# Low parts of x and of weight sums on VectorE instead of GpSimd in eleven steps of an FFT-and-feed-forward kernel

## The chip, the cores and the metric

The kernel runs on one core of a Trainium2 chip. The metric is the device time of one execution in microseconds (us). The engines are named as in the profile: PE is TensorE (PEld its weight loads), ACT is ScalarE, DVE is VectorE, POOL is GpSimd, SP is SyncE, which here issues all DMAs.

## The reference

```python
X = np.fft.rfft(x, axis=1)                     # x: 8 x 3008 x 256
Yr = Xr @ w_r - Xi @ w_i + b_r
Yi = Xr @ w_i + Xi @ w_r + b_i
Y  = soft threshold of Yr and of Yi by 0.01
y  = np.fft.irfft(Y, n=3008, axis=1)           # 8 x 3008 x 256
h  = y.reshape(24064, 256) @ w_in              # w_in: 256 x 2048
out = (h - np.tanh(h)) @ w_out                 # w_out: 2048 x 256
```

## The kernel before

All products run in fp32r. Where one product is not exact enough, a number is split: a high part, cast to fp32r by ACT, and a low part, the number minus its high part. The function `split_into` does this; its last argument names the engine of the low part, and GpSimd is what it takes if nothing is said. The product is then three matmuls: low by high, high by high, high by low.

The transform over 3008 points is done as 64 by 47 points, batch by batch. F1 is the first short transform of a batch. For batch 1 (`Forward`), F1 is done in 16 steps of four matmuls' worth of x each; the last eight of them need x split. A step of F1 has a split (`split`, two slots ahead of its use) and a `part`: three matmuls of 94 x 512, which write a PSUM bank, and a copy by ACT (L278) to `st`, which a DMA writes out.

The feed-forward part works on chunks of 512 tokens. The first three chunks (the first pass) go through a loop of steps g, called slots here. The slots that matter are 31 to 43; 44 begins the main phase. A slot does, in this order of the program:

1. `rise`: six matmuls (L594) into a PSUM bank `he`, the tanh by ACT (L597), the subtraction h - tanh(h) by DVE (L598), which reads `he`, and the cast of its high part by ACT (L599, `ghe`).
2. What the list `slots` holds for this slot, by rank: the F1 part (rank 7), the split of x for the F1 two slots on (8.5), a weight step (9), and where one is due, the stacked table (9, behind the weight steps).
3. `finish`: the low part `gle` by DVE (L603).
4. `fall`: six matmuls (L619) with `ghe` and `gle` of two slots ago.

There are two `he` banks. An F1 part takes one of them too, so that in slots 35 to 42 every `rise` writes the same bank, and its matmuls wait until L598 of the slot before has read it. Every engine runs its own instructions in this order.

`weight_sums(p)` prepares, for each of four groups p, sums of blocks of w_in that the main phase (L698, tile `sum`) uses in place of the blocks. It has four steps: `one` (three additions, DVE), `two` (two more by DVE, and the split of one sum), `three` (the split of a second sum, two operations of DVE), `four` (the split of the third sum, a subtraction by DVE, and the split of its result into the tile `weights`). Groups 0 to 2 stand in slots 33 to 36, 36 to 39 and 39 to 42; group 3 stands in slots 43, 44, 45 and 49. In slots 36 and 39, step four of one group and step one of the next fall together.

The stacked table is a table of the DFT that batches 3 and later use; it is loaded by a DMA and split by three small operations of DVE (L333, L334, L335). Its `f1s_h`, the `ws` tiles of the weight sums and the tile `spare` (L653, an operand that POOL prepares for the main phase from slot 41 on) take turns in four buffers.

Of the kernel before, what the change touches and what calls it, by code (L numbers as in the profile page):

```python
# [78 lines left out]
def spectral_ffn(ctx, tc, x, w_r, w_i, b_r, b_i, w_in, w_out, x_twice, f1, f1s, f2, f2_first, i1, i2, out):  # L79
    nc = tc.nc  # L80
    P = 128
# [16 lines left out]
    def split_into(hi, lo, src, rest=nc.gpsimd):  # L98
        nc.scalar.copy(out=hi, in_=src)  # L99
        rest.tensor_tensor(out=lo, in0=src, in1=hi.bitcast(F32), op=ALU.subtract)  # L100
        return hi, lo
# [236 lines left out]
    def rows(t, jp):  # L338
        return t.rearrange("a (g j) d -> a g (j d)", j=NJ)[:, :, 2 * jp * D:(2 * jp + 2) * D]

    class Spectrum:
# [113 lines left out]
        def put(self, pz):  # L455
            zo = work.tile([P, 512], F32, name="zo", tag="tmp", bufs=4)
            nc.scalar.copy(out=zo, in_=pz)
            nc.sync.dma_start(out=rows(z_dram[self.b], self.jp), in_=zo)
# [60 lines left out]
    def h(t):  # L519
        return t.bitcast(F32)  # L520
# [233 lines left out]
    def weight_sums(p):  # L754
        wv = [weights[p // 2][:, v].rearrange("p (k q i m) -> p k i q m", k=2, i=2, m=P)[:, :, :, 2 * (p % 2):2 * (p % 2) + 2] for v in range(2)]
        pair = [work.tile([P, 2, 2, P], F32, name=f"ws{k}", tag="tmp", bufs=4) for k in range(2)]
        t = [v[:, k] for v in pair for k in range(2)]

        def whole(dst, k, i):
            nc.vector.tensor_tensor(out=dst, in0=h(wv[0][:, k, i]), in1=h(wv[1][:, k, i]), op=ALU.add)  # L760

        def op(dst, a, b, how):
            nc.vector.tensor_tensor(out=dst, in0=a, in1=b, op=how)

        def put_sum(i, src):
            split_into(*(v[:, 2 * p * P:(2 * p + 2) * P].rearrange("p (q m) -> p q m", m=P) for v in sums[i]), src)

        def one():
            whole(t[0], 0, 1)
            whole(t[2], 0, 0)  # L770
            whole(t[1], 1, 1)

        def two():
            op(t[1], t[0], t[1], ALU.add)
            op(t[0], t[2], t[0], ALU.subtract)
            put_sum(2, t[0])

        def three():
            put_sum(0, t[1])
            op(t[3], t[1], t[2], ALU.subtract)  # L780
            whole(t[2], 1, 0)

        def four():
            put_sum(1, t[3])
            op(t[2], t[2], t[3], ALU.subtract)
            split_into(wv[0][:, 0, 1], wv[1][:, 0, 1], t[2])

        return one, two, three, four

# [27 lines left out]
    sums = []  # L817
# [3 lines left out]
    def zero_slot(c):  # L821
        return LAST + 2 + 2 * NP2 * (c - FIRST)

    def busy(slot, us):
        load_at[slot] = load_at.get(slot, 0.0) + us

    def plan_spectrum(b, at, offsets, ahead, earliest):
        shared, cross, shrink, inverse = offsets
        done_at[b] = at[-1] + inverse
        for jp, k in enumerate(at):  # L830
            s = Spectrum(b, jp)
            put(max(k - ahead, earliest), 0, s.load)
            if b > 2:
                put(k - 3, 0.7, s.fix)
            for slot, rank, fn, us in (
                (k, 6, s.dft, 1.8), (k + shared, 4, s.shared, 0.7), (k + cross, 3, s.cross, 1.4),
                (k + shrink, 2, lambda s=s: [s.shrink], 0.3), (k + inverse, 2.5, s.inverse, 0.7),
            ):
                put(slot, rank, fn)
                busy(slot, us)  # L840
            if shared == cross:
                busy(k + shared, 9.0)

    def plan_forward(f, slot, *q):
        if len(q):
            put(slot - 1, 0.5, f.split, *q)
        else:
            put(slot - 2, 8.5, f.split)
        put(slot, 7, f.part, *q)
        busy(slot, 0.8)  # L850
        busy(slot - 1, 0.1)

    def calmest(lo, hi, n, us):
        found = sorted(sorted(range(lo, hi + 1), key=lambda k: (load_at.get(k, 0.0), k))[:n])
        for k in found:
            busy(k, us)
        return found

    def prepare(c):
        chunk = chunks[c]  # L860
        at = zero_slot(c)
        if c > FIRST:
            put(at - 15, 0, chunk.unspill)
        tight = c == first_chunk[1]
        put(at - 4 if tight else at - 5, 9, chunk.sums, 0)
        put(at - 3 if tight else at - 4, 0.9 if tight else 9, chunk.sums, 1)
        put(at - 3, 1, chunk.operands, "t3", "b11", "t2", "b21")
        put(at - 2, 1, chunk.operands, "t1")
        put(at - 2, 9, chunk.sums, 2)
        put(at - 1, 1, chunk.operands, "b22", "t4")  # L870
        busy(at - 3, 1.0)
        busy(at - 1, 0.6)
# [8 lines left out]
    def plan():  # L881
        for p, steps in enumerate(WEIGHT_STEPS):
            for k, at in enumerate(steps):
                put(at, 9, weight_step, p, k)
        put(38, 0, share)
        put(36, 0, table_load)
        put(39, 9, stacked_table)
        put(40, 0, first_spares)
        put(42, 0, operand_tiles)
        put(45, 0, more_operand_tiles)  # L890
        for c in range(FIRST, NCH):
            prepare(c)
        for k, at in enumerate(FIRST_F1):
            ch, q = LOOK + k // 2, k % 2
            if q == 0:
                put(at - AHEAD_F1, 0, following[ch].load)
            put(at - 2, 8.5, following[ch].split, q)
            put(at, 7, following[ch].part, q)
            busy(at, 0.9)
        plan_spectrum(1, SPECTRUM_1, (1, 1, 2, 4), 5, SPECTRUM_1[0] - 2)  # L900
        spectra = [None, None]
        for b in range(2, B):
            zs = zero_slot(first_chunk[b])
            spectra.append(zs - (SHIFT_2 if b == 2 else 89))
            plan_spectrum(b, [spectra[b] + 6 * k for k in range(NJ // 2)], (2, 3, 4, 7), 7, spectra[b] - 3)
        for b in range(2, B):
            zs = zero_slot(first_chunk[b])
            if b == 2:
                at = calmest(F1_2, spectra[b] - 5, NP // 2, 0.8)
            else:  # L910
                first = spectra[b - 1]
                at = [first + 1] + [first + 5 + 6 * k for k in range(12)] + [zs - 111 + 4 * (k + 1) for k in range(3)]
                for k in at:
                    busy(k, 0.8)
            for ch in range(NP // XC if b == 2 else 0):
                f = Forward(b, ch)
                put(at[2 * ch] - 3, 0, f.load)
                for q in range(XC // 2):
                    plan_forward(f, at[2 * ch + q], q)
            for k in range(NP // 2 if b > 2 else 0):  # L920
                f = Stacked(b, 2 * k)
                put(max(at[k] - 6, at[k - 3] - 1 if k > 2 else 0), 0.6, f.load)
                plan_forward(f, at[k])
        for c in range(FIRST + 1, NCH):
            units = [Unit(g // 8, g % 8) for g in range(-(-CT * c // 376), -(-CT * (c + 1) // 376))]
            late = [u for u in units if c == first_chunk[u.b]]
            early = [u for u in units if c != first_chunk[u.b]]
            for some_units, window in ((early, (-14, -9 if late else -6)), (late, (-10, -6))):
                at = unit_slots(c, 2 * len(some_units), window, max([done_at.get(u.b, 0) + 2 for u in some_units], default=0))
                for u in some_units:  # L930
                    mine = [at.pop(0) for _ in range(2)]
                    last_two.append(mine[-1])
                    put(max(mine[0] - 5, 48, done_at.get(u.b, 0) + 1, last_two[-3] + 1), 0, u.load)
                    for k, slot in enumerate(mine):
                        put(slot, 8, u.time, k)
# [18 lines left out]
    def weight_step(p, k):  # L954
        if not sums:
            sums.extend([piece(i + 3 * v, [P, FF // 2], F32R, f"sum{i}_{v}") for v in range(2)] for i in range(3))
        if k == 0:
            wsteps[p] = weight_sums(p)
        wsteps[p][k]()
# [34 lines left out]
    with tc.manual_schedule(engines={E.PE, E.Activation, E.DVE, E.Pool, E.SP}):  # L994
# [27 lines left out]
        for i in range(len(steps) + 1):  # L1022
# [3 lines left out]
            if i < len(steps):  # L1026
                f, q = steps[i]
                f.dft(q)
            if i >= 1:
                f, q = steps[i - 1]  # L1030
# [40 lines left out]
        following = [Forward(1, ch) for ch in range(NP // XC)]  # L1071
# [117 lines left out]

        ready, half = {}, {}  # L1190
        plan()

        def rise(g):
# [119 lines left out]
```

## Time and profile before

| what | value |
|---|---|
| median of 3 runs | 2569.62 us (2569.45 to 2571.41) |
| the profiled execution | 2569.43 us |
| its span (first to last instruction) | 2567.6 us |
| mean granted clock of TensorE | 0.999 of full speed |
| PE busy | 2544.6 us of the span, 99% |
| DVE, ACT, POOL busy | 1837.7, 1598.1 and 787.1 us |

The span is 1.8 us shorter than the execution's own time; this part lies outside of the instructions. A PE that is busy for 99% of the span leaves 23 us in which it stands still.

### The profile page before, as it was taken

The page shows a single profiled execution, that of the slowest core. Times are in us where ns is not written, and L with a number is a line of the kernel's source. Part 1 is how long each engine was busy: PE and PEld are TensorE (multiplying, and loading weights), DVE is VectorE, ACT ScalarE, POOL GpSimd, SP SyncE. Part 2 cuts the span into 40 slices and gives each one's busy share as a digit, 9 for nine tenths or more (in the row PEclk, how much of TensorE's full clock was granted, in tenths as well). Part 3 has the DMA queues.
Part 4 walks back from the last instruction along what each step waited for, and adds up shares of the span by engine and source line. Part 5 has one row for each costly group of instructions (what it writes and reads, how often), then busy time and mean ns, then how long its engine had stood idle before and what let it go on. Part 6 is the DMA issues. An engine that isn't in the chain of part 4 may idle for free.

```text
span 2567.6 us, 42817 instructions
## 1 busy us (share of the span) xinstructions
PE 2544.6 (99%) x16000; PEld 2271.5 (88%) x16000; DVE 1837.7 (72%) x2741; ACT 1598.1 (62%) x2926; POOL 787.1 (31%) x881
## 2 busy tenths in 40 slices
PE   9999999999999999999999999999999999999999
PEld 6787988999899998999989899899998999999998
DVE  6788875777767777777776777767777666666665
ACT  5556567666666666666666666666666555565555
POOL 0004335232343332433333333333333223221210
PEclk9999999999999999999999999999999999999999
DMA  6521224232333332323323242233333121111000
GB/s 181 163 83 53 87 92 125 93 107 86 102 107 105 122 102 86 114 86 123 101 86 117 87 129 91 87 116 103 114 94 96 64 66 60 47 43 47 19 27 17
DMA packets 144528, 232.94 MB, mean 91 GB/s; under 512 B 12096, under 2 KB 85952, under 8 KB 144320
## 3 DMA queue, kind: packets, MB, share of 16 engines
q1 hardware_dynamic: 144320, 230.20, 28.8%
q8 instruction: 127, 2.08, 0.3%
q14 instruction: 81, 0.66, 0.1%
HBM read 139.45 MB, written 87.56 MB: 88 GB/s over the span
## 4 chain that ended last, share of the span: by engine, by line
PE 95%; DVE 2%; ACT 1%; DMA 1%; issue 0%; POOL 0%; SPq 0%; ACTq 0%; POOLq 0%; DVEq 0%
PE o L619 39%; PE H L698 34%; PE ps_v L403 5%; PE ps_i L545 4%; PE ps_f L376 3%; PE ps_t L403 2%; PE he L594 2%; PE ps_f L314 1%; PE ps_i L452 1%; PE ps_i L450 1%; PE ps_i L451 1%; PE oe L619 1%; PE ps_f L258 0%; PE ps_v L485 0%; DVE the L598 0%
## 5 line engine op out<-in xcount | busy, mean ns | idle before, releaser
L619 PE MATMUL o<-gh,weights 128*128 128x512 f32 x2816 | 886.2, 396 | 0.0
L742 ACT CAST gh<-th 128x1024 fp32r<-128x1024 f32 x353 | 371.5, 1053 | 382.2 <-DVE th L737 252.9
L698 PEld LDWEIGHTS H<-y_t,sum 128*128 128x128 f32 x3168 | 516.4, 188 | 102.7 <-DVE th L737 5.7
L619 PE MATMUL o<-gl,weights 128*128 128x512 f32 x1408 | 554.4, 394 | 0.0
L698 PE MATMUL H<-y_t,sum 128*128 128x256 f32 x3168 | 548.5, 281 | 0.3
L747 DVE TENSOR_TENSOR gl<-th,gh 128x1024 fp32r<-128x1024 f32 x353 | 440.6, 1249 | 57.1 <-ACT gh L742 54.0
L619 PEld LDWEIGHTS o<-gh,weights 128*128 128x128 f32 x2816 | 442.0, 188 | 14.9
L737 DVE TENSOR_TENSOR th<-H,th 128x1024 f32<-128x1024 f32 x353 | 428.4, 1214 | 5.3 <-ACT th L733 2.3
L733 ACT ACTIVATE th<-H 128x1024 f32<-128x1024 f32 x353 | 362.5, 1027 | 41.3 <-PE H L698 40.8
L714 DVE TENSOR_TENSOR H<-H,late 128x256 f32<-128x256 f32 x352 | 152.2, 432 | 317.3 <-PE H L698 281.5
L698 PE MATMUL H<-y_b,weights 128*128 128x256 f32 x2112 | 361.5, 279 | 0.0
L619 PEld LDWEIGHTS o<-gl,weights 128*128 128x128 f32 x1408 | 264.8, 188 | 60.0 <-DVE gl L747 0.6
L698 PE MATMUL H<-y_more,weights 128*128 128x256 f32 x2112 | 308.7, 281 | 1.2 <-DVE H L720 1.2
L698 PEld LDWEIGHTS H<-y_b,weights 128*128 128x128 f32 x2112 | 298.5, 188 | 0.2 <-POOL y_b L100 0.2
L698 PEld LDWEIGHTS H<-y_more,weights 128*128 128x128 f32 x2112 | 282.3, 188 | 15.9 <-DVE H L720 1.9
L720 DVE TENSOR_TENSOR H<-H,late 128x256 f32<-128x256 f32 x352 | 151.7, 431 | 191.0 <-PE H L698 182.8
L706 ACT COPY late<-H 128x256 f32<-128x256 f32 x352 | 131.6, 374 | 213.1 <-PE H L698 210.1
L100 POOL TENSOR_TENSOR z_l<-mn,z_h 128x512 fp32r<-128x512 f32 x84 | 112.7, 1342 | 431.6 <-ACT z_h L99 277.1
L440 DVE TENSOR_TENSOR y<-tb,ps_v 64x256 f32<-64x256 f32 x384 | 160.7, 418 | 50.5 <-PE ps_v L403 44.0
L100 POOL TENSOR_TENSOR s_l<-xi,s_h 128x256 fp32r<-128x256 f32 x84 | 62.8, 748 | 319.0 <-ACT s_h L99 319.0
L309 POOL TENSOR_TENSOR x<-x,x 64x512 fp32r<-64x512 f32 x55 | 71.4, 1298 | 254.2 <-ACT x L303 105.2
L707 ACT COPY H<-H 128x256 f32<-128x256 f32 x352 | 125.7, 357 | 11.2
(194 smaller groups left out, 3590.3 us busy)
## 6 DMA issues: line engine op xcount, KB each, us to landing
a<-st SPq DMA_DIRECT2D x168, 192.0 KB
x<-in_x_twice SPq DMA_DIRECT2D x55, 512.0 KB
z<-zo SPq DMA_DIRECT2D x96, 256.0 KB
zin<-z SPq DMA_DIRECT2D x64, 384.0 KB
out<-ot SPq DMA_DIRECT2D x46, 512.0 KB
at<-a SPq DMA_DIRECT2D x84, 256.0 KB
shared<-a SPq DMA_DIRECT2D x60, 256.0 KB
shared<-in_i SPq DMA_DIRECT2D x58, 235.0 KB
```

The lines of the kernel that those rows point to most:

```text
L100: rest.tensor_tensor(out=lo, in0=src, in1=hi.bitcast(F32), op=ALU.subtract)
L403: nc.tensor.matmul(dst, lhs[:, t], rhs[:, t, :], start=n == 0, stop=n == 5)
L440: nc.vector.tensor_tensor(out=y[ri * 64:(ri + 1) * 64, jj, :], in0=common(jj, ri), in1=self.vv[jj * 64:(jj + 1) * 64, ri * D:(ri + 1) * D] ...
L619: nc.tensor.matmul(self.o[t][:, :n], lhs, rhs, start=f == 0 and k == 0, stop=f == NF - 1 and k == 2,)
L698: nc.tensor.matmul(dst, a, b, start=start and k == 0, stop=k == 2, skip_group_check=True)
L706: nc.scalar.copy(out=self.p7, in_=self.c11)
L714: nc.vector.tensor_tensor(out=self.c21, in0=self.acc, in1=self.p7, op=ALU.add)
L720: nc.vector.tensor_tensor(out=self.c22, in0=self.acc, in1=self.p7, op=ALU.add)
L733: nc.scalar.activation(out=self.th[:, s], in_=self.hp[:, s, :n], func=AF.Tanh)
L737: nc.vector.tensor_tensor(out=self.th[:, s], in0=self.hp[:, s, :self.n], in1=self.th[:, s], op=ALU.subtract)
L742: nc.scalar.copy(out=self.gh[:, s], in_=self.th[:, s])
L747: nc.vector.tensor_tensor(out=self.gl[:, s], in0=self.th[:, s], in1=h(self.gh[:, s]), op=ALU.subtract)
```

## The change

```diff
+        rest = nc.gpsimd if p == 3 else nc.vector
...
         def put_sum(i, src):
-            split_into(*(v[:, 2 * p * P:(2 * p + 2) * P].rearrange("p (q m) -> p q m", m=P) for v in sums[i]), src)
+            split_into(*(v[:, 2 * p * P:(2 * p + 2) * P].rearrange("p (q m) -> p q m", m=P) for v in sums[i]), src, rest)
...
         def four():
             put_sum(1, t[3])
             op(t[2], t[2], t[3], ALU.subtract)
-            split_into(wv[0][:, 0, 1], wv[1][:, 0, 1], t[2])
+            split_into(wv[0][:, 0, 1], wv[1][:, 0, 1], t[2], rest)
...
         put(38, 0, share)
-        put(36, 0, table_load)
-        put(39, 9, stacked_table)
+        put(27, 0, table_load)
+        put(31, 9, stacked_table)
...
             if q == 0:
                 put(at - AHEAD_F1, 0, following[ch].load)
-            put(at - 2, 8.5, following[ch].split, q)
+            put(at - 2, 8.5, following[ch].split, q, None, nc.vector)
             put(at, 7, following[ch].part, q)
```

Twenty subtractions go from POOL to DVE: eight low parts of x (slots 33 to 40), and for groups 0 to 2 nine low parts of sums and three of `weights`. The table is loaded in slot 27 and split in slot 31, in place of 36 and 39. Lines below the first edit move by two: L760 becomes L762, L763 becomes L765.

On DVE, slot 36 (step four of group 0 and step one of group 1) stood so before, from the L598 of its own `rise` to the next:

```order
L598 TENSOR_TENSOR the_978<-he0_973,the_978 128x512
L763 TENSOR_TENSOR ws1_1731<-ws1_1731 128x256
L760 TENSOR_TENSOR ws0_1827<-weights0_78 128x256
L760 TENSOR_TENSOR ws1_1828<-weights0_78 128x256
L760 TENSOR_TENSOR ws0_1827<-weights0_78 128x256
L603 TENSOR_TENSOR gle_982<-the_978,ghe_980 128x512
L598 TENSOR_TENSOR the_978<-he0_973,the_978 128x512
```

The same slot of the change:

```order
L598 TENSOR_TENSOR the_978<-he0_973,the_978 128x512
L100 TENSOR_TENSOR x_1_5_1_l_1824<-xt_1707,x_1_5_1_h_1823 94x512
L100 TENSOR_TENSOR sum1_1_1734<-ws1_1738,sum1_0_1733 128x256
L765 TENSOR_TENSOR ws1_1738<-ws1_1738 128x256
L100 TENSOR_TENSOR weights0_78<-ws1_1738,weights0_78 128x2x128
L762 TENSOR_TENSOR ws0_1832<-weights0_78 128x256
L762 TENSOR_TENSOR ws1_1833<-weights0_78 128x256
L762 TENSOR_TENSOR ws0_1832<-weights0_78 128x256
L603 TENSOR_TENSOR gle_982<-the_978,ghe_980 128x512
L598 TENSOR_TENSOR the_978<-he0_973,the_978 128x512
```

Three subtractions of L100 stand between the two L598; each reads a high part that ACT casts in this slot.

On ACT the order is the same before and after. This is slot 36 of the change, from its tanh to the next:

```order
L597 ACTIVATE the_978<-he0_973 128x512
L599 CAST ghe_980<-the_978 128x512
L278 COPY st_1820<-he1_974 96x512
L99 CAST x_1_5_1_h_1823<-xt_1707 94x512
L99 CAST sum1_0_1733<-ws1_1738 128x256
L99 CAST weights0_78<-ws1_1738 128x2x128
L597 ACTIVATE the_978<-he0_973 128x512
```

Nothing moved here; the casts that the three subtractions read stand behind L599 and L278.

On POOL, the queue of the change holds behind the one early operation of the preparation (L132) at once the operands of the main phase:

```order
L132 TENSOR_TENSOR w2_f_256<-wi_f_125,wr_f_124 128x512
L653 TENSOR_TENSOR spare_1950<-raw_960 128x256
L653 TENSOR_TENSOR raw_960<-raw_960 128x256
L653 TENSOR_TENSOR spare_1950<-raw_960 128x256
L100 TENSOR_TENSOR y_t3_2009<-spare_1950,y_t3_2009 128x256
```

Before, 18 low parts stood ahead of the first L653, and two more between the second and the third.

## Rows read from the trace of the kernel before

**Rows 1.** Windows: length, then busy us and instructions by engine, clock, DMA.

```profile
200.00:250.00 50.00, 44.65 (x191) 33.98 (x190) 41.92 (x68) 30.07 (x63) 25.65 (x27) 1.00 0.17 48
250.00:300.00 50.00, 48.35 (x329) 44.22 (x328) 39.97 (x68) 30.06 (x60) 16.02 (x19) 1.00 0.30 96
300.00:2500.00 2200.00, 2197.35 (x14260) 1989.39 (x14259) 1561.14 (x2262) 1392.09 (x2543) 738.20 (x822) 1.00 0.29 90
```

**Rows 2.** Waits of PE in 180 to 310 us: total us, times, longest us.

```profile
PE he L594 <- DVE the L598: 4.2, 3, 1.7
```

**Rows 3.** Timeline of DVE, 196 to 262 us: start us, us, instruction [idle before].

```profile
207.06 0.69 DVE L598 TENSOR_TENSOR the<-he,the 128x512 f32<-128x512 f32 x1 [0.32 <-ACT the L597]
207.66 0.68 DVE L212 TENSOR_TENSOR weights<-w_m,weights 128x512 fp32r<-128x512 f32 x1
...
217.63 0.69 DVE L598 TENSOR_TENSOR the<-he,the 128x512 f32<-128x512 f32 x1 [1.09 <-ACT the L597]
...
219.09 1.08 DVE L760 TENSOR_TENSOR ws<-weights 128x256 f32<-128x256 f32 x3
220.10 0.68 DVE L603 TENSOR_TENSOR gle<-the,ghe 128x512 fp32r<-128x512 f32 x1
...
223.73 2.47 DVE L603 TENSOR_TENSOR gle<-the,ghe 128x512 fp32r<-128x512 f32 x1
...
231.84 1.98 DVE L334 CAST f1s_h<-f1s_f 128x48 fp32r<-128x48 f32 x1
...
235.65 0.41 DVE L763 TENSOR_TENSOR ws<-ws 128x256 f32<-128x256 f32 x1
236.09 0.42 DVE L763 TENSOR_TENSOR ws<-ws,ws 128x256 f32<-128x256 f32 x1
236.44 0.68 DVE L603 TENSOR_TENSOR gle<-the,ghe 128x512 fp32r<-128x512 f32 x1
...
245.07 0.69 DVE L598 TENSOR_TENSOR the<-he,the 128x512 f32<-128x512 f32 x1 [1.27 <-ACT the L597]
```

**Rows 4.** Timeline of POOL, 190 to 262 us.

```profile
223.54 1.41 POOL L100 TENSOR_TENSOR x_l<-xt,x_h 94x512 fp32r<-94x512 f32 x1
224.92 0.73 POOL L100 TENSOR_TENSOR sum<-ws,sum 128x256 fp32r<-128x256 f32 x1
...
241.36 0.73 POOL L653 TENSOR_TENSOR spare<-raw 128x256 f32<-128x256 f32 x1
```

**Rows 5.** Timeline of ACT, 196 to 262 us: slot 36.

```profile
218.36 0.62 ACT L599 CAST ghe<-the 128x512 fp32r<-128x512 f32 x1 [0.76 <-DVE the L598]
218.88 0.58 ACT L278 COPY st<-he 96x512 f32<-96x512 f32 x1
219.36 0.62 ACT L99 CAST x_h<-xt 94x512 fp32r<-94x512 f32 x1
219.88 0.41 ACT L99 CAST sum<-ws 128x256 fp32r<-128x256 f32 x1
```

**Rows 6.** Line L100 by engine, DVE: min, median, max ns, first and last start.

```profile
L100 DVE TENSOR_TENSOR x_l<-xt,x_h x2: 682/686/690, 81.4 to 87.6; 94x512 fp32r<-94x512 f32 x2
L100 DVE TENSOR_TENSOR f_l<-f_f,f_h x1: 255/255/255, 4.4 to 4.4; 94x96 fp32r<-94x96 f32 x1
```

**Rows 7.** Timeline of PE, 196 to 262 us.

```profile
213.19 0.40 PE L619 MATMUL o<-gle,weights 128*128 128x512 f32 x1
...
218.80 1.09 PE L594 MATMUL he<-yh,weights 128*128 128x512 f32 x4
...
222.28 1.08 PE L594 MATMUL he<-yh,weights 128*128 128x512 f32 x4
...
245.82 1.20 PE L594 MATMUL H<-yh,weights 128*128 128x512 f32 x4
```

**Rows 8.** Timeline of PE, 19 to 36 us: the end of its longest wait.

```profile
26.50 2.63 PE L376 MATMUL ps_f<-f_f,at 128*128 128x128 f32 x16 [3.81 <-DMA at<-a_first]
```

**Rows 9.** A window of 1 us (columns as in rows 1), behind that wait.

```profile
28.00:29.00 1.00, 1.00 (x7) 1.00 (x6) 0.42 (x1) 0.25 (x1) 0.00 (x0) 0.50 0.67 163
```

## What is expected of the change, and why

> **What bounds the kernel now.** I read the windows first, to see where PE stands still. The 50 us from 200 us on hold 44.65 us of PE work, so 5.35 us of idle PE; the next 50 us hold 48.35; the following 2200 us lack only 2.65 us [rows 1]. From 300 us on PE is the bound, and an idle microsecond of PE ahead of it moves the end by a microsecond. The change lies in 200 to 250 us. Then the waits: 4.2 us of this idle time are three waits of the `rise` matmuls (L594) for DVE's L598, the longest 1.7 us [rows 2]. That is the single `he` bank of slots 35 to 42: the next `rise` can't write before L598 has read. So I follow L598 and call the time from one L598 to the next a round. Slots 33 to 42 are ten rounds, from 207.06 to 245.07 (eleven L598 in all): 38.01 us [rows 3]. The matmuls of the main phase's first `rise` start at 245.82, 0.75 behind the last of these L598 [rows 7]. Whatever the ten rounds gain or lose, the end does too.
>
> How long must a round be? PE needs 3.48 us for a slot with F1: from one `rise` at 218.80 to the next at 222.28, with nothing idle between [rows 7]. Several rounds of before are longer, and the DVE timeline shows why: a subtraction that mostly takes 0.68 us takes 2.47 at 223.73 [rows 3], while POOL is busy with a subtraction from 223.54 and the next one to 225.65 [rows 4]; it ends at 226.20, about one normal duration behind POOL. L334, a cast of 128x48, takes 1.98 [rows 3].
>
> **The change, part by part.**
>
> *Removed.* The stretching by POOL goes. If nothing took its place, PE would get back at most the 4.2 us of waits for L598 [rows 2].
>
> The Trainium skill, page "SBUF — State Buffer", section "Who interferes with whom", says that a DVE instruction with two SBUF inputs contends with a GpSimd instruction that reads SBUF, and that the loser blocks fully. The rows on 223.73 agree. By that rule alone the change is a gain; it is the first rival below.
>
> *Added.* Twenty subtractions on DVE. Eight are 94x512: two such on DVE have a median of 686 ns [rows 6], and behind an instruction of that width the next starts after 0.60 (207.06 to 207.66) [rows 3]. Twelve are 128x256; 0.34 each, a third of the 1.01 from the three L760 to L603 (219.09 to 220.10) [rows 3]. As work this is 8 x 0.60 + 12 x 0.34 = 8.9 us in ten rounds. But the price is not the work. Each subtraction reads a high part that ACT casts late in the same slot, and now DVE waits for it, with L603 and the next L598 queued behind. On POOL nobody waited.
>
> How late ACT is, I read from slot 36, whose L598 starts at 217.63 [rows 3]. ACT then starts L599 at 218.36, the F1 copy at 218.88, the cast of x at 219.36 and the cast of the sum at 219.88 [rows 5]. Counted from L598 that is +0.73, +1.25, +1.73 and +2.25. The cast of x takes 0.62, so it ends at +2.35; with 0.03 to hand over, the low part of x starts at +2.38 and DVE goes on at +2.98. Before, DVE went on to its weight step at once. A cast of 256 columns takes 0.41 [rows 5]; a weight operation that reads the result of the one before starts 0.44 behind it and takes 0.41 (235.65, 236.09) [rows 3]. With that each new round, every handover 0.03:
>
> - Step three (slots 35, 38): the cast of the sum is done by +2.66, so the low part runs at once; 2.98 + 0.34, then 0.44 + 0.34 for its two operations, 0.60 for L603: 4.70.
> - Step two (37, 40): 2.98 + 0.44, the second operation done at 3.83, cast of the sum to 4.27, low part from 4.30 to 4.64, L603: 5.24.
> - Steps four and one together (36, 39): 2.98 + 0.34 = 3.32, the subtraction done at 3.73, cast for `weights` to 4.17, low part from 4.20 to 4.54, three additions 1.01, L603: 6.15.
> - Slot 33 (step one; a weight cast stands where the F1 copy does later): 3.02 + 1.01 + 0.60 = 4.63. Slot 34 (step two, no F1 copy): 0.48 less than in 37, so 4.76.
> - Slot 41 (three, no x left): cast of the sum from +1.73 to 2.14, low part to 2.51, 0.78, L603: 3.89. Slot 42 (four): 2.51, done at 2.92, cast to 3.36, low part to 3.73, L603: 4.33.
>
> Sum: 4.63 + 4.76 + 2 x 4.70 + 2 x 5.24 + 2 x 6.15 + 3.89 + 4.33 = 49.79 us, against 38.01: **+11.8 us**. All these rounds are longer than PE's 3.48, so none of it is covered by PE's work. The tanh that L598 also needs is no later than this: PE may start the next `rise` 0.75 behind L598 [rows 7], and ACT is free again when the last cast is done, one L603 and more ahead.
>
> *Moved: the table.* In slot 39 its three operations cost 1.98 us and more, which is in the 38.01 already. In slot 31 they stand ahead of L603 and L598, where POOL is idle. Upper bound: three times the 255 ns of a subtraction twice as wide [rows 6], 0.77; lower bound 0. I take half: **+0.4**. The DMA of the table is issued in slot 27, four slots ahead; I cost it at nothing, hidden behind those slots.
>
> *Freed: POOL.* L653 now stands first in POOL's queue and waits only for its tile `spare`, whose buffer is given up in slot 38. So three L653 of 0.73 each [rows 4] come about slot 38 or 39 and can hold up DVE there: 0 to 2.2 us. DVE idles for ACT in most of that time, so I take one of them: **+0.7**.
>
> Together 11.8 + 0.4 + 0.7 = 12.9. On the profiled execution's 2569.43 us (0.2 below the median of the runs) this gives **2582.3 us**, 0.5% slower.
>
> **The rivals.**
>
> *Faster: DVE doesn't wait for ACT.* If the casts were ready when DVE reaches them, a round would be its own work: step three 0.60 + 0.60 + 0.34 + 0.44 + 0.34 + 0.60 = 2.92, below PE's 3.48, and the 4.2 us of waits go, less 0.4 for the table: 2565.6. It decides at rounds of 3.48. For it speaks the stretching [rows 3, 4]. Against it, x is cast behind L599 and the F1 copy, which the change doesn't move; L599 itself can't start before L598 ends. Chance 0.07.
>
> *Partly covered.* The waits overlap more than I count, or the 1.65 us that PE idles in 250 to 300 us [rows 1] and later idle time is absorbed by the delay. If a round lost half of what I say, +6 us: 2575.5; near zero if more. Chance 0.10, half of it within 0.2% of before, which is about what a measurement of this kernel can tell from no change (5 us).
>
> *Slower still: TensorE's clock falls.* Its slots 33 and 34 pass at PE's pace, since there the `he` banks still alternate; then PE meets the first long round. PE's last `fall` of slot 35 began its last matmul at 213.19 [rows 7]; with 0.4 for the table and 0.4 for that matmul it is through at 214.0, while the new L598 of slot 35 starts at 207.06 + 0.4 + 4.63 + 4.76 = 216.85 and frees the bank 0.75 later, at 217.6: a wait of 3.6 us. Before, behind a wait of 3.81 us that ended at 26.50 [rows 8] the granted clock was 0.50, the 1.2 GHz level, from 28 to 29 us [rows 9]. One such dip is covered: the `rise` of 1.4 us becomes 2.8, in a round where DVE is later anyway. If the clock stayed at the lower level through slots 35 to 42, a slot would need 2 x 3.48 = 6.96, and the excess over my rounds is 2 x (2.26 + 0.81 + 1.72) + 3.07 + 2.63 = 15.3: 2597.6. In 200 to 250 us the clock stayed at 1.00 with idle PE of up to 1.7 us at a time [rows 1, 2], which speaks against it; the other new waits are some 1 to 2.7 us each. Chance 0.06.
>
> **How the numbers follow.** My forecast has 0.77, the faster rival 0.07, partly covered 0.10, the clock 0.06. The forecast's own range is 2579.5 to 2585: the table 0 to 0.77, L653 0 to 2.2, 1.65 us that may come back later, and ten rounds at 0.1 each for handovers. With 0.23 left to the others, the range for 8 in 10 takes in the nearer part of "partly covered" and of a clock that stays low for a few slots: 2576.5 to 2587. Slower by over 0.2%: 0.77 + 0.06 + half of 0.10 = 0.88; same 0.05; faster 0.07.
>
> **What would show it.** In the changed profile L598 should come every 4.6 to 6.2 us in slots 33 to 40, with DVE idle up to a microsecond per slot "until ACT x_h" and again until the casts of sums; no DVE instruction there much over 0.69 us except one or two beside L653; the waits of `rise` for L598 about 15 us in place of 4.2, the longest near 3.6; POOL empty up to L653; and the table's three operations under 0.8 us together. I am wrong if DVE finds the casts done, so that L598 follows at PE's pace, or if rounds show clock below 1.00.

## The result: 0.5% slower, as forecast

| | before | the change |
|---|---|---|
| median | 2569.53 us (2568.35 to 2571.41) | 2583.03 us (2582.06 to 2583.92) |
| profiled execution, and its span | 2569.43, 2567.6 us | 2583.86, 2582.1 us |
| PE busy in the span | 2544.6 us | 2551.9 us |
| DVE, ACT, POOL busy | 1837.7, 1598.1, 787.1 us | 1839.2, 1598.5, 766.9 us |

The ratio is 1.0051 [1.0039, 1.0062], 13.5 us between the medians; forecast were 2582.3 us. POOL lost 20 us of work and DVE gained 1.5, so the busy times tell nothing of a loss of 13.5 us.

The ten rounds of slots 33 to 42 tell more. Columns of the windows: start and end, length, then busy us and instructions of PE, PEld, DVE, ACT and POOL, granted clock, DMA share, GB/s. Before:

```profile
207.06:245.07 38.01, 32.77 (x138) 24.79 (x137) 31.68 (x49) 23.77 (x49) 21.58 (x22) 1.00 0.19 54
```

The same ten rounds of the change, and three stretches within them:

```profile
207.29:257.74 50.45, 39.30 (x140) 27.77 (x138) 32.60 (x66) 24.16 (x49) 2.62 (x3) 0.90 0.14 40
...
220.00:225.00 5.00, 5.00 (x19) 3.90 (x18) 3.28 (x8) 1.93 (x4) 0.00 (x0) 0.78 0.46 128
...
229.00:232.00 3.00, 3.00 (x9) 2.16 (x8) 1.55 (x4) 1.45 (x4) 0.00 (x0) 0.50 0.24 66
...
245.00:250.00 5.00, 5.00 (x15) 3.71 (x15) 2.88 (x6) 2.48 (x5) 0.00 (x0) 0.66 0.14 41
```

They take 50.45 us in place of 38.01: +12.44. DVE did 17 instructions more (the twenty, less the table's three) and was busy only 0.92 us longer: the added work is about what the stretching by POOL, that of the table's operations included, had cost. So DVE stood still 17.85 us instead of 6.33. What for, the waits of DVE in 205 to 262 us say (total us, times, longest us):

```profile
DVE x_l L100 <- ACT x_h L99: 11.9, 8, 1.7
DVE sum L100 <- ACT sum L99: 4.4, 5, 1.5
DVE weights L100 <- ACT weights L99: 1.4, 3, 0.5
DVE the L598 <- ACT the L597: 1.0, 2, 0.7
```

The first three lines, 17.7 us, are low parts that wait for their high parts. The two waits of the last line lie at the edges of the stretch (0.32 at 207.29 and 0.69 at 261.32): from the first of the ten rounds to the last, no L598 waited for its tanh. One round shows how. This is the timeline of DVE in the change (start, duration, idle before and what ended it): slot 36, and the L603 of slot 38.

```profile
221.42 0.68 DVE L598 TENSOR_TENSOR the<-he,the 128x512 f32<-128x512 f32 x1
223.79 0.69 DVE L100 TENSOR_TENSOR x_l<-xt,x_h 94x512 fp32r<-94x512 f32 x1 [1.69 <-ACT x_h L99]
224.40 0.41 DVE L100 TENSOR_TENSOR sum<-ws,sum 128x256 fp32r<-128x256 f32 x1
224.74 0.41 DVE L765 TENSOR_TENSOR ws<-ws 128x256 f32<-128x256 f32 x1
225.62 0.42 DVE L100 TENSOR_TENSOR weights<-ws,weights 128x256 fp32r<-128x256 f32 x1 [0.47 <-ACT weights L99]
225.97 1.09 DVE L762 TENSOR_TENSOR ws<-weights 128x256 f32<-128x256 f32 x3
226.97 0.69 DVE L603 TENSOR_TENSOR gle<-the,ghe 128x512 fp32r<-128x512 f32 x1
227.57 0.68 DVE L598 TENSOR_TENSOR the<-he,the 128x512 f32<-128x512 f32 x1
...
236.95 1.22 DVE L603 TENSOR_TENSOR gle<-the,ghe 128x512 fp32r<-128x512 f32 x1
```

And the timeline of ACT in the same slot:

```profile
222.14 0.62 ACT L599 CAST ghe<-the 128x512 fp32r<-128x512 f32 x1 [2.21 <-DVE the L598]
222.66 0.57 ACT L278 COPY st<-he 96x512 f32<-96x512 f32 x1
223.14 0.62 ACT L99 CAST x_h<-xt 94x512 fp32r<-94x512 f32 x1
223.66 0.40 ACT L99 CAST sum<-ws 128x256 fp32r<-128x256 f32 x1
```

The low part of x starts 2.37 us behind L598, 0.03 behind the end of its cast (223.76), and the round is 6.15 us long. The loop goes through both engines: ACT's L599 waits for L598 (2.21 us idle), the cast of x stands behind L599 and L278, and the next L598 stands behind the subtraction.

Waits of PE in the change, 180 to 325 us, where [rows 2] had 4.2 us in three:

```profile
PE he L594 <- DVE the L598: 8.4, 4, 2.5
PE H L594 <- DVE the L598: 1.3, 1, 1.3
...
PE he L261 <- DVE the L598: 0.9, 1, 0.9
```

The first `rise` of the main phase starts at 258.48 in place of 245.82 [rows 7]: +12.66 of the 14.5 us by which the span is longer. The other 1.8 come 140 us later and are told below.

### The profile page after: what moved, and what is told of

The parts are those of the page before. It is cut to its first block, busy times and chain, and to the rows that moved or that the text cites. A ratio compares the mean times of both kernels' runs of the same rounds, so it can differ in the third digit from the quotient of the medians.

```text
span 2582.1 us, 42804 instructions
## 1 busy us (share of the span) xinstructions
PE 2551.9 (99%) x16000; PEld 2275.3 (88%) x16000; DVE 1839.2 (71%) x2761; ACT 1598.5 (62%) x2926; POOL 766.9 (30%) x861
## 4 chain that ended last, share of the span: by engine, by line
PE 94%; DVE 2%; ACT 1%; DMA 1%; issue 1%; POOL 0%; SPq 0%; POOLq 0%; ACTq 0%
PE o L619 39%; PE H L698 34%; PE ps_v L403 4%; PE ps_i L545 4%; PE ps_f L376 3%; PE ps_t L403 2%; PE he L594 2%; PE ps_f L314 1%; PE ps_i L452 1%; PE ps_i L450 1%; PE ps_i L451 1%; PE oe L619 1%; PE ps_f L258 0%; DVE the L598 0%; PE ps_v L485 0%
## 5 line engine op out<-in xcount | busy, mean ns | idle before, releaser
L698 PEld LDWEIGHTS H<-y_t,sum 128*128 128x128 f32 x3168 | 516.3, 188 | 102.6 <-DVE th L737 5.7
L698 PE MATMUL H<-y_t,sum 128*128 128x256 f32 x3168 | 548.3, 281 | 0.3
L619 PEld LDWEIGHTS o<-gh,weights 128*128 128x128 f32 x2816 | 441.9, 188 | 14.9
L698 PE MATMUL H<-y_b,weights 128*128 128x256 f32 x2112 | 361.5, 279 | 0.0
L698 PE MATMUL H<-y_more,weights 128*128 128x256 f32 x2112 | 308.7, 281 | 1.1 <-DVE H L720 1.1
L698 PEld LDWEIGHTS H<-y_b,weights 128*128 128x128 f32 x2112 | 298.5, 188 | 0.2 <-POOL y_b L100 0.2
L698 PEld LDWEIGHTS H<-y_more,weights 128*128 128x128 f32 x2112 | 282.4, 188 | 15.8 <-DVE H L720 1.9
L100 POOL TENSOR_TENSOR z_l<-mn,z_h 128x512 fp32r<-128x512 f32 x84 | 112.7, 1342 | 431.7 <-ACT z_h L99 283.1
L100 POOL TENSOR_TENSOR s_l<-xi,s_h 128x256 fp32r<-128x256 f32 x84 | 62.8, 748 | 318.7 <-ACT s_h L99 318.7
L707 ACT COPY H<-H 128x256 f32<-128x256 f32 x352 | 125.7, 357 | 11.2
```

The lines of the kernel that those rows point to most:

```text
L619: nc.tensor.matmul(self.o[t][:, :n], lhs, rhs, start=f == 0 and k == 0, stop=f == NF - 1 and k == 2,)
L698: nc.tensor.matmul(dst, a, b, start=start and k == 0, stop=k == 2, skip_group_check=True)
```

## The experiments

The theory: DVE, in order, waits for casts that ACT makes late, and the next L598 stands behind. Its rivals: it is the amount of work on DVE; it is TensorE's lower clock; it is the table. Times of before were taken anew beside each group of runs: 2569.28 us beside the first four, 2568.77 beside the next three, 2569.09 beside the last. In the kernels with later subtractions, lines are numbered up to nine higher: L607 is L598, L612 L603, L606 L597, L707 L698, L772 L765 and L769 L762; L261 and L782 are the later low parts of x and of sums, L781 the casts of sums.

### Each part by itself

The split of x and the table as in the change, the weight sums back on POOL:

```diff
-        rest = nc.gpsimd if p == 3 else nc.vector
+        rest = nc.gpsimd
```

> Only the eight low parts of x go to DVE (and the table moves); the low parts of the sums stay on POOL. Theory (DVE waits in its queue for casts that ACT makes late in the slot): a round of slots 33 to 40 still has the cast of x on its path, so x_l starts 2.38 us behind L598 as in the change; the waits for the casts of sums go, but POOL's subtractions of 0.74 can hold up DVE again. 6 to 11 us over before: 2576 to 2581. Rival (the added DVE work is the price, wherever it stands): 4.8 of 8.9 us of work, so 4.8/8.9 of the 13.5 us: about 2577. This run alone does not separate the two by its time; the start of x_l behind L598 does.

Measured: 2577.46 us, 1.003 [1.0019, 1.004], +8.2 us. Timeline of DVE in this kernel, slot 36:

```profile
220.62 0.69 DVE L598 TENSOR_TENSOR the<-he,the 128x512 f32<-128x512 f32 x1
222.99 0.69 DVE L100 TENSOR_TENSOR x_l<-xt,x_h 94x512 fp32r<-94x512 f32 x1 [1.69 <-ACT x_h L99]
...
224.94 1.21 DVE L603 TENSOR_TENSOR gle<-the,ghe 128x512 fp32r<-128x512 f32 x1
```

The same 2.37 us between L598 and the low part, though the sums are gone from DVE: it is the place of the cast that decides. The time alone would not have told this from the work, since both came to about 2577. POOL's stretching is back as well, if smaller (1.21 here, 2.47 in [rows 3]).

The weight sums and the table as in the change, the split of x back on POOL:

```diff
-            put(at - 2, 8.5, following[ch].split, q, None, nc.vector)
+            put(at - 2, 8.5, following[ch].split, q)
```

> Only the twelve low parts of sums and weights go to DVE (and the table moves); those of x stay on POOL. Theory: each of the twelve waits for its cast, and that cast stands on ACT behind the cast of x, so a round is hardly shorter than in the change; POOL's 1.3 us for x can hold up DVE in the same place. 5 to 14 us over before: 2575 to 2584. Rival (work alone): 4.1 of 8.9 us of work, about 6 us over before: 2576.

Measured: 2581.14 us, 1.0046 [1.0032, 1.006], +11.9 us. DVE now waits 13.8 us in nine waits for casts of sums, up to 2.0 us at a time: the cast of the sum stands on ACT behind that of x. Timeline of DVE, slot 36 of this kernel:

```profile
220.04 0.68 DVE L598 TENSOR_TENSOR the<-he,the 128x512 f32<-128x512 f32 x1
222.71 1.31 DVE L100 TENSOR_TENSOR sum<-ws,sum 128x256 fp32r<-128x256 f32 x1 [1.99 <-ACT sum L99]
```

The sum's low part starts 2.67 behind L598 and takes 1.31 beside POOL's subtraction of x (0.41 without). The twelve small subtractions, 12 x 0.34 = 4.1 us of work, cost 11.9: work alone doesn't give that. The two parts are 8.2 and 11.9 alone and 13.5 together: whoever waits for the cast of x finds the cast of the sum nearly done, so the two waits overlap. The ten rounds alone say the same: 45.97 us with x alone and 49.97 with the sums alone, 8.0 and 12.0 over before.

The table alone (the subtractions as before):

```diff
-        put(36, 0, table_load)
-        put(39, 9, stacked_table)
+        put(27, 0, table_load)
+        put(31, 9, stacked_table)
```

> Only the table moves; all low parts stay on POOL. Theory: the table costs 0.4 us in slot 31 and frees up to 2 us in slot 39, where POOL may still hold up L603: 2568 to 2570, no change that can be told. Rival (the table in its new place delays the last weight blocks and with them PE): several us slower, 2574 or more.

Measured: 2568.76 us, 0.9997 [0.9989, 1.0006]: no difference that can be measured. The loss doesn't come from the table.

### The same work, one slot later

All twenty subtractions stay on DVE. ACT makes the casts where it did, but each low part is put into the next slot, behind L598, when its cast is long done. The edit is against the change; `lows` is a list that `put_lows` works off.

```diff
+            nc.scalar.copy(out=hi, in_=src)
+            lows.append(lambda: nc.vector.tensor_tensor(out=lo, in0=src, in1=h(hi), op=ALU.subtract))
...
+        for at in range(35, 44):
+            put(at, 0.6, put_lows)
...
-            put(at - 2, 8.5, following[ch].split, q, None, nc.vector)
+            put(at - 2, 8.5, following[ch].split_high, q)
+            put(at - 1, 0.5, following[ch].split_low, q)
```

> The same twenty subtractions on DVE as in the change, and the table where the change has it, but each subtraction stands one slot later in DVE's queue, ahead of the weight step, when ACT's cast is long done. Theory (the wait for casts is the price): DVE's work per slot is at most about 3.5 us, PE's pace, so the rounds fall to 3.5 to 3.7 us, the waits of PE for L598 go below 1.5 us, and the time is 2565.5 to 2568, faster than before. Rival (the added work on DVE is the price): as the change, about 2583.

Measured: 2568.26 us, 0.9995 [0.9986, 1.0003], 0.3 us above the range that was expected, and not told from before. The same instructions on the same engine cost 13.5 us in one order and nothing that can be measured in the other: the work as the cause is out. Timeline of DVE, slot 37 of this kernel, where the low parts of slot 36 stand now:

```profile
219.99 0.69 DVE L607 TENSOR_TENSOR the<-he,the 128x512 f32<-128x512 f32 x1
220.60 0.68 DVE L261 TENSOR_TENSOR x_l<-xt,x_h 94x512 fp32r<-94x512 f32 x1
221.20 0.41 DVE L782 TENSOR_TENSOR sum<-ws,sum 128x256 fp32r<-128x256 f32 x1
221.53 0.41 DVE L782 TENSOR_TENSOR weights<-ws,weights 128x256 fp32r<-128x256 f32 x1
...
223.71 0.69 DVE L607 TENSOR_TENSOR the<-he,the 128x512 f32<-128x512 f32 x1 [0.37 <-ACT the L606]
```

No gap stands ahead of a low part any more, and the round is 3.72 us where it was 5.27; that of slot 36 is 3.49 where it was 6.15. The ten rounds take 34.90 us, 3.1 less than before. Of that 1.0 us is left in the total, less than its interval can tell from nothing; the waits of PE in this kernel, 180 to 310 us, show the main reason (the longest):

```profile
PE H L707 <- DVE ot L650: 1.7, 1, 1.7
```

The waits for L598 are down to 1.2 us, but in slot 43 DVE is now late: the last low parts stand there ahead of three additions (1.64 for 1.09) and L603 (1.21), both stretched beside POOL, and a copy that PE needs (L650, `ot`) comes late. This 1.7 us and 0.44 for the table, which stands ahead of the ten rounds, make up the difference between 3.1 and 1.0.

### Half of it later

Only x one slot later, the sums where the change has them:

```diff
-            lows.append(lambda: nc.vector.tensor_tensor(out=lo, in0=src, in1=h(hi), op=ALU.subtract))
+            nc.vector.tensor_tensor(out=lo, in0=src, in1=h(hi), op=ALU.subtract)
```

> All twenty subtractions on DVE as in the change; the eight of x stand one slot later, those of the sums where the change has them. Theory (rounds follow from the waits for casts, by the same arithmetic as the prediction): without the wait for x, step three 4.41 (the cast of the sum still ends 2.66 behind L598), steps four and one together 5.86, step two 3.63; slots 33 to 42 come to 43.0, with 0.5 for the operands that POOL prepares 43.5, against 50.45 in the change: 7 us less, about 2576. Rival (work alone): as the change, 2583.

The edit is against the kernel with all low parts later. Measured: 2575.22 us, 1.0022 [1.0013, 1.0031], +6.5 us; the ten rounds take 44.20 us.

Only the sums one slot later, x where the change has it:

```diff
-            put(at - 2, 8.5, following[ch].split_high, q)
-            put(at - 1, 0.5, following[ch].split_low, q)
+            put(at - 2, 8.5, following[ch].split, q, None, nc.vector)
```

> All twenty on DVE; the twelve of sums and weights stand one slot later, those of x where the change has them. Theory: the wait for x remains (2.98 behind L598 before DVE goes on); steps three and two 4.36, four and one together 4.93, slots 41 and 42 at PE's pace of 3.3 to 3.5; slots 33 to 42 come to 42.6, with 0.5 for POOL's operands 43.1: 7.4 us less than the change, about 2575.5. Rival (work alone): as the change, 2583.

Measured: 2577.54 us, 1.0032 [1.002, 1.0045], +8.8 us, 2 us more than expected (the edit is again against the kernel with all low parts later); the ten rounds take 44.62 us, 1.5 more than expected. DVE and ACT show where the larger part of this arises. Timeline of DVE in this kernel, the L598 that ends slot 37:

```profile
231.01 0.69 DVE L607 TENSOR_TENSOR the<-he,the 128x512 f32<-128x512 f32 x1 [0.37 <-ACT the L606]
```

Timeline of ACT there:

```profile
230.07 0.41 ACT L781 CAST sum<-ws 128x256 fp32r<-128x256 f32 x1 [1.55 <-DVE ws L772]
230.38 0.59 ACT L606 ACTIVATE the<-he 128x512 f32<-128x512 f32 x1
```

The cast of the sum waits for DVE's weight step, the tanh of the next slot stands behind that cast on ACT, and L598 waits for the tanh: 4.82 us for step two (slots 37 and 40) where 4.36 was expected. Of the 8.8 us, 6.6 are in the ten rounds; the wait of PE for `ot`, 1.7 us, is here too, since the last low parts stand in slot 43 as in the kernel with all low parts later. Taking the subtraction away from DVE doesn't free the round when its producer still stands in ACT's queue behind a late weight step.

This kernel also bears on the clock. Its window over these rounds:

```profile
205.00:260.00 55.00, 42.62 (x175) 30.52 (x174) 40.52 (x79) 30.43 (x64) 7.98 (x8) 1.00 0.16 47
```

The clock stayed at 1.00, PE's 2.4 GHz, and the rounds still lost 6.6 us. So waiting loses such times without any help from the clock.

Set against its own before, the change lies 13.5 us above it, with x later 6.5, with the sums later 8.8, with both later 1.0 below: moving x gives back 7.0 us, moving the sums 4.7, moving both 14.5. Both kernels with the sums later also have the wait for `ot`; the ten rounds alone, which don't hold it, give back 6.3, 5.8 and 15.6 us. The two waits overlap here too.

### A version that uses it

Later low parts for all, the table back in slots 36 and 38, and the last low parts late in slot 44:

```diff
+        for at in range(35, 44):
+            put(at if at < 43 else 44, 0.6 if at < 43 else 9.5, put_lows)
...
-        put(27, 0, table_load)
-        put(31, 9, stacked_table)
+        put(36, 0, table_load)
+        put(38, 9, stacked_table)
```

> As the run with all twenty subtractions one slot later (2568.3), with the table loaded in slot 36 and split in slot 38, where DVE has time left, and the last two low parts behind the weight step of slot 44 in place of slot 43, where they delayed a copy (L641 before the edits) for which PE waited 1.7 us. Theory: 0.4 and about 1.2 us less, 2566 to 2567.5, by 0.1% faster than before, which the measurement may just not tell. Rival (those two waits are covered anyway): 2568.3.

Measured: 2566.40 us, 0.9992 [0.9983, 1.0001]: just not told from no change. The same kernel once more:

> The kernel of the run before once more, for its interval only: 2566 to 2567.5, 0.05 to 0.13% below the kernel before.

Measured: 2565.77 us, 0.9988 [0.9979, 0.9997], a little below what was expected. Waits of PE for L598 come to 1.3 us there, and that for `ot` is gone. It is some 0.1% below before and 0.6% below the change: moving the subtractions off POOL, with the table split in slot 38 for 39, measured 2.4 and 3.3 us less than before, of the 4.2 us of waits in [rows 2], once the low parts come when their inputs are there. What the table's slot has in this was not tried by itself, and the first of the two intervals takes in no change.

## Why the prediction was right, step by step

*The bound.* A wait for L598 moves the end: right. The rounds grew by 12.44 us and the main phase began 12.66 later. The difference is the table's 0.44, less the 0.20 by which this execution was ahead at the L598 of slot 31 (199.68 against 199.88). To this point the forecast was 12.9.

*The rounds.* Forecast against measured: slot 33 4.63 and 4.63; 34 4.76 and 4.79; 35 4.70 and 4.71; 36 6.15 and 6.15; 37 5.24 and 5.27; 38 4.70 and 5.25; 39 6.15 and 6.15; 40 5.24 and 5.27; 41 3.89 and 3.89; 42 4.33 and 4.34. The one that is off by more than 0.03 is slot 38, and there L653 was costed apart.

*POOL freed.* Forecast: one L653 lengthens a DVE instruction by 0.7 about slot 38 or 39. The timeline of POOL in the change:

```profile
236.79 0.83 POOL L653 TENSOR_TENSOR spare<-raw 128x256 f32<-128x256 f32 x1 [216.80 <-DVE ws L765]
```

POOL had been empty for 216.80 us. While this L653 and the next ran, L603 took 1.22 in place of 0.69 (236.95 above), and the round was 0.54 longer than that of slot 35. The forecast size was a little too high. The Trainium skill, page "SBUF — State Buffer", section "Who interferes with whom", says that a DVE instruction with two SBUF inputs contends with a GpSimd instruction that reads SBUF, and that such contention is an exclusive lock. The 1.22 here and the 1.31 for 0.41 of the kernel with the sums alone on DVE agree. The stretching by POOL did go, as the first rival had it, but what took its place cost more.

*The table.* 0.44 measured (0.4 forecast), from the first cast to L603 in the timeline of DVE:

```profile
203.86 0.18 DVE L333 CAST f1s<-f1s_f 128x48 fp32r<-128x48 f32 x1
...
204.30 0.69 DVE L603 TENSOR_TENSOR gle<-the,ghe 128x512 fp32r<-128x512 f32 x1
```

*What was off: PE's waits.* Forecast for `rise` were 15 us with a longest of 3.6; there are 9.7 and 2.5 (10.6 with the 0.9 of an F1 matmul). Two things were missed. The timeline of PE at slots 35 and 36 of the change:

```profile
212.66 0.47 PE L261 MATMUL he<-x_h,f_l 94*96 94x512 f32 x1 [0.92 <-DVE the L598]
212.97 0.39 PE L262 MATMUL he<-x_h,f_h 94*96 94x512 f32 x1
213.19 0.39 PE L263 MATMUL he<-x_l,f_h 94*96 94x512 f32 x1
...
214.58 0.40 PE L619 MATMUL o<-gle,weights 128*128 128x512 f32 x1
217.45 1.20 PE L594 MATMUL he<-yh,weights 128*128 128x512 f32 x4 [2.47 <-DVE the L598]
...
219.09 0.63 PE L261 MATMUL he<-x_h,f_l 94*96 94x512 f32 x1
219.52 0.63 PE L262 MATMUL he<-x_h,f_h 94*96 94x512 f32 x1
```

The F1 matmuls of slot 35 need the other `he` bank, and already waited 0.92 us for the L598 of slot 34; the prediction took PE to be through at 214.0, and it was so near 215. The `rise` itself came where L598 put it (217.6 forecast, 217.45). And behind this wait the clock fell, as in the rival: the F1 matmuls of slot 36 start 0.43 apart, those of slot 35 still 0.31 and 0.22 (212.66, 212.97, 213.19). The windows above show granted clocks of 0.50, the 1.2 GHz level, and of 0.78 and 0.66, means of stretches at the 2.4 and the 1.2 GHz level; it fell three times in the ten rounds, behind waits of 2.47, 2.07 and 2.40 us. A part of what would have been idle thus shows as busy PE: of the 12.44 us, PE was busy for 6.53 and idle for 5.91. The prediction named two signs of being wrong. One of them, "if rounds show clock below 1.00", came: that the clock would hold but for one covered dip was wrong. It did not set the length of these rounds: each is as long as DVE and ACT make it by the arithmetic at full clock, and no L598 waited for its tanh. The rival in which the clock stays low and decides (2597.6) didn't come.

*What was not foreseen: the last 1.8 us of the profiled execution.* Some payback of up to 1.65 us was allowed for; there was a loss. At the first transform of a result, the timeline of PE in the change and, below it, before:

```profile
396.52 3.38 PE L545 MATMUL ps_i<-shared,zin 128*128 128x141 f32 x12 [2.41 <-DMA zin<-z]
```

```profile
383.39 1.84 PE L545 MATMUL ps_i<-shared,zin 128*128 128x141 f32 x12 [1.71 <-DMA zin<-z]
```

The wait for the transfer is 0.70 longer and the twelve matmuls 1.54. The windows of 396 to 398 and 398 to 400 us show 0.56 and 0.58 of the clock there. With the 12.66 this is 14.9, and 0.4 is gained elsewhere. It goes with the execution: in the eight other profiles with waits of 1.2 to 1.7 us here, the experiments' and before's, the matmuls took 1.84; in one of the best version's two, with 2.30, 3.35. The change's four times lie near 2582.1 and 2583.9, which would fit a wait that is long in some executions only; why it is long in these was not tried and stays open. So the 13.5 us between the medians may hold some of a loss that was not forecast; what the prediction had right is the 12.66 ahead of the main phase.

## What to carry to other kernels

An instruction moved from an engine for which nobody waits to one that sets a loop's pace is priced by when its inputs come, not by how long it runs: here 8.9 us of work, which replaced as much stretching, made ten rounds some 12 us longer by waiting. Look up on the producing engine's timeline when the input is ready, counted from the loop's own beat, and put the consumer behind that, if need be a round later; the engine's busy time hardly changes, its idle time does. When two waits overlap, taking either away gives back less than its own length, and undoing one part at a time doesn't add up.

## What the runs showed of the hardware

The granted clock fell to the 1.2 GHz level behind waits of PE of 2 to 3 us, but not behind all of them. It fell behind 2.47, 2.07 and 2.40 us in the rounds of the change (waits that ended at 217.45, 228.31 and 244.98), behind 2.41 later in it (396.52) and behind 2.30 at that place in one profile of the best version. It held behind 2.02 us with x alone on DVE and behind 2.03 with the sums later. With x later it fell behind 2.11 us (240.69) and held behind 2.10 (226.24). With the sums alone on DVE it fell at waits of 2.03 and 2.99 us (215.49 and 244.09) and held at another of 2.99, as PE and the window there show:

```profile
227.52 1.20 PE L594 MATMUL he<-yh,weights 128*128 128x512 f32 x4 [2.99 <-DVE the L598]
```

```profile
227.00:232.00 5.00, 3.76 (x15) 2.66 (x15) 3.74 (x6) 2.42 (x5) 1.29 (x1) 1.00 0.14 39
```

So the length of the one wait doesn't decide it here. Behind waits of up to 1.7 us, in the ten rounds and at the first transform of a result, no profile shows a fall.

A DVE subtraction beside one on POOL took 1.2 to 1.3 us where 0.4 to 0.7 is usual (236.95 in the change, 224.94 and 222.71 in the first two experiments); 2.47 in [rows 3] was beside two of POOL's in a row.
